# Another written-out order for a fused sliding-window attention and token mixer on one core

## The chip, the core and the metric

The kernel runs on one core of one Trainium2 chip. The metric is the device time of one execution in microseconds (us); a time below is the median of several runs where it says so. The engines are TensorE (PE in the profile, with its weight loads as PEld), VectorE (DVE), ScalarE (ACT), GpSimd (POOL) and SyncE (SP). TensorE's results go to PSUM, which the kernel takes as four pairs of banks, `pair` 0 to 3.

## The reference

Inputs are q, k and v of shape (8 batches, 8 heads, 576 positions, 64), the weights `w_q` and `w_k` (512 x 64) and `w_out` (512 x 512); the output is (8, 576, 512), all in float32. Attention looks back over a window of 128 positions, with a bias that is linear in the distance; a mixer over the positions of each batch follows.

```python
scores = scale * np.matmul(q, k.transpose(0, 1, 3, 2))      # scale = 1/8
bias = slopes[:, None, None] * (-np.abs(rel))[None]         # slopes 2**-(h+1)
mask = (rel >= 0) & (rel < 128)
scores = np.where(mask, scores + bias[None], -1000000000.0)
attn = exp(scores - max) / sum
x = (attn @ v), heads side by side                          # (8, 576, 512)
wq, wk = x @ w_q, x @ w_k                                   # (8, 576, 64)
W_tok = scale * np.einsum('bsd,btd->bst', wq, wk)
mixed = np.einsum('bst,btd->bsd', W_tok, x)
out = np.maximum(mixed, 0.0) @ w_out
```

## The kernel before

**The work of one batch.** The loads bring q, k and v into SBUF as fp16 (the DMA converts). TensorE transposes q (TQ), k (TK) and the last 64 rows of both (TT, for two batches at once); copies bring the transposed blocks from PSUM to the tile `qkT` (ETQ, ETK, ETT). Batch 0 has forms of its own for its first blocks: float32 loads by the queues of ACT and SP (LF), transposes TF and TJ, copies EF and EJ. For each of four groups of 128 keys, g, and each half of the heads, u, QKb.g.u makes the scores in a pair of banks, and EXPb.g.u on ACT writes their exponential to a tile `pt`; MULb.g on DVE multiplies both halves by the exponential of bias and mask, made once at the start. PVb.t multiplies by v, with a column of ones that gives the sums; RC takes their reciprocal and X the product, both on DVE. So one batch is eight QK, eight EXP, four MUL, and five each of PV, RC and X.

**The mixer of two batches.** It works on the pairs of batches (0, 1), (2, 3), (4, 5) and (6, 7), and an operation is named after the first of the two. XT and XTT transpose x, EXT and EXTT copy it out; WQ, WK and WT project it, with copies EWQ, EWK and EWT; G multiplies wk by x (copy EG), MX that by wq, so that the matrix of 576 x 576 is never made. RM and RMT are the relu. OUTb.t multiplies by `w_out` (five for a batch, the last, OUTb.4, for both batches of the pair), EO copies the result to an SBUF tile `osb`, and DO stores it. The very last output, OUT7.3, is made in two halves, a and b.

**What sets the order.** The program keeps no schedule of its own: a function declares each operation with what it depends on, and `ORDER`, one long text, lists all of them in the order of issue. A word such as `ETQ5:D` names the operation and the engine; `TQ5:P3` puts a product on TensorE into the pair 3, and `OUT7.4:P11` into the second bank of pair 1. `Order.follow` reads the text, and each engine has its operations in that order; between engines the semaphores follow from the data and the banks. An engine therefore waits at an operation whose data isn't there, with everything behind it. Copies that may run on ACT or DVE get their engine from the text, and `cp` writes them (L245 for ACT, L247 for DVE; where both sides are fp16, ACT is given pairs of values as float32). EXP, MUL, RC and X always have the same engine, and so the loads L378 to L404, which POOL issues one after the other to one DMA queue.

**Tiles.** There are three sets of buffers for k, two for q, four for v, six `pt`, two `qkT`, 20 `osb`. A load into a buffer waits for the last user of what it held. The stores of the first two pairs of batches all go through SP, and in both orders they stand behind DO3.0, one of the last of them: they are held until then.

**Zero products.** `WARM` gives the sizes of groups of products of a zero tile (WM.0 and on) whose results nobody reads; the order puts them where it likes on TensorE.

Of the kernel before, what the change touches and what calls it, by code (L numbers as in the profile page):

```python
# [15 lines left out]
S = 576  # L16
D = 64
# [46 lines left out]
QK2.1.0:P2 ETT2:D Lv2.1:G EXP2.1.1:A ETT3:D WK0:P10 MUL2.0:D Lv2.2:G EXP2.1.0:A XTT0:P0 QK2.3.0:P3
EXTT0:D WQ0:P11 Lv2.3:G EWK0:A MUL2.1:D EXP2.3.0:A QK2.3.1:P0 TQ3:P2 Lq4.0:G MUL2.2:D EXP2.3.1:A
Lwo0:G WT0:P10 ETQ3:D PV2.0:P0 EWT0:A Lwo1:G TK3.0:P3 ETK3.0:A G0:P10 RC2.0:D Lk4.1:G X2.0:D
MUL2.3:D EWQ0:A Lk4.0:G TK3.1:P3 EG0:A QK3.0.0:P0 EXP3.0.0:A Lv3.0:G ETK3.1:D MX0.0:P1 QK3.0.1:P2
RM0.0:D MX0.1:P3 EXP3.0.1:A Lv3.1:G MX0.3:P0 Lq5.01:G RM0.3:D RM0.1:A PV2.1:P1 QK3.1.0:P2 RC2.1:D
PV2.2:P3 EXP3.1.0:A X2.1:D MX0.2:P0 RC2.2:D QK3.3.1:P1 RM0.2:A X2.2:D PV2.3:P2 Lq5.02:G MUL3.0:D
QK3.1.1:P3 EXP3.3.1:A XT2.0:P00 PV2.4:P01 RC2.3:D EXP3.1.1:A Lq5.03:G X2.3:D TQ4:P1 RC2.4:D EXT2.0:A  # L70
X2.4:D QK3.2.1:P3 ETQ4:D OUT0.2:P20 Lq5.00:G EXP3.2.1:A XT2.1:P21 Lv3.2:G MUL3.1:D EO0.2:A
QK3.2.0:P1 TK4.0:P3 Lv3.3:G EXP3.2.0:A QK3.3.0:P0 ETK4.0:D OUT0.1:P20 Lk5.0:G EXT2.1:D EXP3.3.0:A
QK4.0.1:P1 MUL3.2:D QK4.1.1:P3 Lk5.1:G OUT1.3:P21 EXP4.1.1:A Lv3.4:G MUL3.3:D PV3.0:P0 EO0.1:A
PV3.1:P3 Lk4.3:G EXP4.0.1:A OUT1.1:P20 RC3.1:D RC3.0:D X3.1:D Lk4.2:G EO1.3:A QK4.1.0:P1 X3.0:D
TQ5:P3 EXP4.1.0:A Lt2:G MX0.4:P0 XT3.0:P21 ETQ5:D RMT0:A PV3.2:P1 EO1.1:A PV3.3:P0 Lv5.0:G RC3.2:D
EXT3.0:A X3.2:D OUT1.2:P20 Lv4.0:G RC3.3:D X3.3:D QK4.0.0:P1 TK5.0:P3 Lv4.1:G EXP4.0.0:A XT3.1:P21
ETK5.0:D PV3.4:P00 Lk5.3:G EO1.2:A QK5.1.0:P3 RC3.4:D QK5.0.1:P1 X3.4:D EXP5.1.0:A OUT0.0:P20
Lv4.2:G EXT3.1:D MUL4.0:D EXP5.0.1:A QK5.0.0:P0 Lk5.2:G TK4.1:P3 OUT0.3:P21 EXP5.0.0:A Lk6.0:G
ETK4.1:D TT4:P1 EO0.0:D EO0.3:A Lq6.02:G XTT2:P3 QK5.1.1:P0 ETT5:D ETT4:A OUT1.0:P20 EXTT2:D Lk6.2:G
EXP5.1.1:A MUL4.1:D PV4.0:P3 Lk6.1:G QK4.2.0:P1 EO1.0:A QK4.2.1:P0 RC4.0:D WK2:P21 EXP4.2.0:A X4.0:D  # L80
Lv5.1:G MUL5.1:D OUT1.4:P20 EXP4.2.1:A Lk6.3:G PV4.1:P1 MUL5.0:D EWK2:A Lq6.01:G EO1.4:A TK5.1:P0
# [6 lines left out]
TK7.0:P1 QK6.1.0:P3 Lv5.4:G ETK7.0:D OUT3.3:P20 EXP6.1.0:A RC4.4:D Lv5.3:G X4.4:D QK6.1.1:P1
MUL5.2:D QK6.2.1:P0 QK6.2.0:P3 Lv7.3:G EXP6.1.1:A OUT2.1:P21 Lk7.2:G EXP6.2.0:A XT5.0:P10 OUT2.3:P11
Lk7.3:G EO2.1:A EXT5.0:D EXP6.2.1:A MUL5.3:D PV5.2:P3 Lv6.2:G OUT2.2:P10 EO3.3:A Lv6.0:G RC5.2:D  # L90
EO2.3:A X5.2:D TT6:P2 EO2.2:A TQ7:P0 Lv6.1:G ETT6:D QK6.0.1:P3 ETT7:D QK6.0.0:P1 ETQ7:D Lv6.3:G
EXP6.0.1:A PV5.4:P20 OUT3.2:P21 Lv6.4:G EXP6.0.0:A RC5.4:D MUL6.1:D QK6.3.0:P0 Lv7.0:G PV5.3:P3
EXP6.3.0:A OUT3.1:P10 X5.4:D Lv7.4:G RC5.3:D EO3.2:A X5.3:D Lv7.2:G QK6.3.1:P0 EO3.1:A QK7.1.0:P2
# [59 lines left out]
def kernel(  # L153
# [915 lines left out]
```

## Time and profile before

| | |
|---|---|
| time, median of 3 runs | 136.86 us (136.12 to 137.25) |
| the profiled execution | 136.26 us, of which the span of the trace 134.2 us |
| granted TensorE clock | 1.00 |
| busy TensorE | 122.3 us |
| busy VectorE | 114.1 us |
| busy ScalarE | 103.2 us |
| busy GpSimd (issuing the loads) | 86.3 us |
| first exponential to last exponential | 10.09 to 104.23 us |
| PV7.0, one of the last products of the attention | 109.91 us |
| last product on TensorE | ends at 130.16 us |

Times within the trace count from the start of the span. A row of a group gives the line, the engine, the operation, the written tile, the read tiles and the number of instructions, then the busy time and the mean in ns of one, then the idle time of the engine just ahead of them and what ended most of it. A row of the timeline gives the start, the length, the engine, the line, and the instruction, with how many follow each other. A row of stretches gives for each engine, in the order PE, PEld, DVE, ACT, POOL, its busy time and its instructions, and then the granted clock, the mean number of busy DMA engines and the GB/s. Lines are those of the kernel before.

### The profile page before, as it was taken

What the parts mean: (1) busy time and instruction counts of PE and PEld (TensorE: products, weight loads), DVE (VectorE), ACT (ScalarE), POOL (GpSimd) and SP (SyncE); (2) the same over time, 40 slices, a digit from 0 to 9 for tenths busy, and PEclk for the clock granted to TensorE, in tenths of its full rate; (3) what the DMA queues carried; (4) which work ended last, traced back from release to release, by engine and by line L of the source; (5) the groups of instructions that cost most, each with busy time, mean ns of one, the idle gap of its engine ahead of it and who ended that gap; (6) DMA issues with size and microseconds to landing.
All of it is one profiled execution on the core that took longest, in us unless ns stands there. A gap on an engine that the chain in (4) does not pass through costs nothing.

```text
span 134.2 us, 5053 instructions
## 1 busy us (share of the span) xinstructions
PE 122.3 (91%) x2176; PEld 77.2 (58%) x2176; DVE 114.1 (85%) x197; ACT 103.2 (77%) x145; POOL 86.3 (64%) x108
## 2 busy tenths in 40 slices
PE   6988767889999799999999999999999999999970
PEld 2545545766676475576576675565685576634440
DVE  5746899999999999998999999699999999557830
ACT  2579898945998898988999999999999931367040
POOL 7997989499999659899999999999000000000000
PEclk9999999999999999999999999999999999999999
DMA  3999999999999999999999999999929895758894
GB/s 90 222 171 171 157 154 178 167 158 153 162 165 159 195 188 155 157 154 157 154 157 155 157 158 152 152 155 153 100 88 358 317 363 215 230 151 323 275 364 150
DMA packets 105414, 24.97 MB, mean 186 GB/s; under 512 B 95536, under 2 KB 100912, under 8 KB 105392
## 3 DMA queue, kind: packets, MB, share of 16 engines
q0 software_dynamic: 96832, 14.42, 151.6%
q1 hardware_dynamic: 6688, 9.44, 20.7%
q10 hardware_dynamic: 1872, 0.79, 2.2%
q8 instruction: 17, 0.28, 0.8%
q14 instruction: 5, 0.04, 0.1%
HBM read 29.62 MB, written 9.44 MB: 291 GB/s over the span
## 4 chain that ended last, share of the span: by engine, by line
PE 59%; DMA 16%; DVE 9%; ACT 6%; POOL 3%; issue 3%; ACTq 0%; POOLq 0%; DVEq 0%
PE pair L231 48%; DMA natq<-in_q_dram 12%; PE pair L234 11%; DMA natk<-in_k_dram 4%; ACT pt L654 4%; DVE pt L666 3%; DVE qkT L247 3%; DVE rm L882 2%; POOL natk L378 1%; DVE x L727 1%; ACT rm L880 1%; POOL vt L404 1%; POOL natq L382 1%; ACT wqT L245 0%; ACT gs L245 0%
## 5 line engine op out<-in xcount | busy, mean ns | idle before, releaser
L654 ACT ACTIVATE pt<-pair 128x1024 f16<-128x1024 f32 x64 | 62.9, 1032 | 8.0 <-PE pair L231 7.6
L666 DVE TENSOR_TENSOR pt<-pt,bias 128x2048 f16<-128x2048 f16 x32 | 38.5, 1217 | 0.4 <-ACT pt L654 0.3
L404 POOL DMA_DIRECT2D vt<-in_v_dram x40 | 35.1, 949 | 2.4 <-DMA vt<-in_v_dram 1.2
L231 PE MATMUL pair<-wout_sb,rm 128*128 128x512 f16 (+1 forms) x132 | 31.7, 373 | 0.0
L378 POOL DMA_DIRECT2D natk<-in_k_dram x31 | 28.5, 943 | 2.3 <-DMA natq<-in_q_dram 1.7
L231 PE MATMUL pair<-vt,pt 128*128 128x65 f16 (+1 forms) x576 | 22.2, 194 | 2.2 <-DVE pt L666 0.6
L231 PEld LDWEIGHTS <-pt 128*128 128x128 f16 (+1 forms) x576 | 19.2, 100 | 8.0 <-issue 3.5
L245 ACT COPY osb<-pair 128x512 f32<-128x512 f32 (+1 forms) x24 | 13.9, 593 | 11.4 <-PE pair L231 5.8
L727 DVE TENSOR_TENSOR x<-pair,inv 128x512 f16<-128x512 f32 x32 | 21.8, 690 | 0.9
L231 PE MATMUL pair<-qkT 64*128 64x256 f16 (+2 forms) x320 | 22.1, 250 | 0.4 <-DVE qkT L247 0.2
L247 DVE COPY qkT<-pair 128x1024 f16<-128x1024 f16 (+2 forms) x27 | 19.4, 736 | 3.6 <-PE pair L234 3.5
L231 PEld LDWEIGHTS <-rm 128*128 128x128 f16 x132 | 11.4, 97 | 12.1 <-issue 2.2
L231 PEld LDWEIGHTS <-qkT 64*128 64x128 f16 x320 | 10.6, 94 | 8.3 <-issue 2.8
L247 DVE COPY osb<-pair 128x512 f32<-128x512 f32 (+1 forms) x13 | 8.7, 668 | 5.1 <-PE pair L231 5.1
L390 POOL DMA_DIRECT2D natq<-in_q_dram x12 | 11.1, 949 | 1.8 <-PE pair L231 1.6
L880 ACT ACTIVATE rm<-pair 128x1024 f16<-128x1024 f32 x11 | 11.1, 1041 | 0.5 <-PE pair L231 0.3
L234 PE MATMUL pair<-identh,x 128*128 128x128 f16 x128 | 9.9, 220 | 0.0
L231 PE MATMUL pair<-warm 128*128 128x512 f16 x24 | 8.0, 450 | 1.6 <-DVE warm L316 1.2
L234 PEld LDWEIGHTS <-x 128*128 128x128 f16 x128 | 7.5, 98 | 2.3 <-issue 1.3
L247 DVE COPY xT<-pair 128x1024 f16<-128x1024 f16 x11 | 7.5, 686 | 1.2 <-PE pair L234 1.1
L234 PE MATMUL pair<-identh,natk 64*128 64x64 f16 x248 | 6.9, 191 | 1.4 <-ACT qkT L245 0.6
L234 PE MATMUL pair<-identh,natq 128*64 128x128 f16 (+2 forms) x256 | 6.9, 206 | 0.9 <-DMA natq<-in_q_dram 0.9
(68 smaller groups left out, 129.3 us busy)
## 6 DMA issues: line engine op xcount, KB each, us to landing
out_dram<-osb SPq DMA_DIRECT2D x30, 256.0 KB, 3.0
vt<-in_v_dram POOLq DMA_DIRECT2D x32, 128.0 KB, 6.2
natk<-in_k_dram POOLq DMA_DIRECT2D x31, 128.0 KB, 5.9
natq<-in_q_dram POOLq DMA_DIRECT2D x4, 512.0 KB, 7.8
natq<-in_q_dram POOLq DMA_DIRECT2D x12, 128.0 KB, 5.7
out_dram<-osb SPq DMA_DIRECT2D x9, 128.0 KB, 2.4
vt<-in_v_dram POOLq DMA_DIRECT2D x8, 64.0 KB, 5.6
natt<-in_q_dram POOLq DMA_DIRECT2D x4, 128.0 KB, 6.0
```

Source lines behind the costliest of these rows:

```text
L231: hold(nc.tensor.matmul(*a, **k))
L234: hold(nc.tensor.transpose(*a))
L245: hold(nc.scalar.copy(out_ap, in_ap))
L247: hold(nc.vector.tensor_copy(out=out_ap, in_=in_ap))
L378: return lambda: nc.gpsimd.dma_start(out=natk(b, n), in_=k[b, :, P * n:P * n + P, :].transpose([1, 0, 2]))
L390: return lambda: nc.gpsimd.dma_start(out=rows_q(b)[:, r], in_=q[b, :, 0:512, :].rearrange("h (p r) d -> r p h d", r=QR)[r])
L404: return lambda: nc.gpsimd.dma_start(out=vtv(b, t)[:n, :, 0:D], in_=v[b, :, P * t:P * t + n, :].transpose([1, 0, 2]))
L654: nc.scalar.activation(out=pt, in_=two(s.bank).rearrange("p e c -> p (e c)"), func=AF.Exp, scale=SCALE)
L666: nc.vector.tensor_tensor(out=pv, in0=pv, in1=bt, op=ALU.mult)
L727: nc.vector.tensor_tensor(out=x_s[b % NX][qt].rearrange("p (g h d) -> p g h d", g=2, h=4), in0=sums(p)[:, :, :, 0:64], in1=box["inv"].unsq ...
L880: hold(nc.scalar.activation(out=out_ap, in_=in_ap, func=AF.Relu, scale=WSCALE))
L882: hold(nc.vector.tensor_scalar(out=out_ap, in0=in_ap, scalar1=0.0, scalar2=WSCALE, op0=ALU.max, op1=ALU.mult))
```

## The change

`ORDER` is another text for the same operations, and `WARM` has three groups of zero products, 15 in all, where there were eight, 24 in all. All line numbers behind `ORDER` grow by one. Nothing else differs.

- **First loads.** LF0.0.0.0 goes from ACT's queue to SP's and LF0.0.1.0 the other way. The other first blocks of batch 0 (TF0.1.0) are transposed first, and the zero products stand behind the first of these transposes: seven, then two and six later, where twelve stood around TF0.0.0 and twelve, singly or in pairs and threes, further on.
- **Copies.** From DVE to ACT go ETQ1, ETQ3, ETQ4 and ETQ5; ETK2.0, 2.1, 5.0, 5.1, 7.0 and 7.1; ETT5 and 6; EXT0.0, 1.1, 4.1, 5.1, 6.0 and 7.0; EXTT2; RM0.0 and 0.3; EWT6 and EWQ6; eight EO. From ACT to DVE go EF0.1.0, ETT0 and ETT4, EXT2.0 and 6.1, EXTT4, RM0.1, 0.2 and 6.0, EWQ0, EWQ2 and EWT2, EG6, and nine EO with both halves of OUT7.3 then on DVE. A fill of a constant tile changes its place too.
- **Loads.** POOL issues the same 96 loads in another order. Lk1.0 is the first, Lv2.4 goes from the first place to the 43rd, and the slices of the queries of batches 5 to 7 (Lq) and the tails (Lt) stand elsewhere among the others.
- **The end.** The MULs of batch 7 come in the order 1, 3, 2, 0 instead of 1, 0, 3, 2, and EXP7.0.0 is the last EXP where EXP7.2.0 was; XTT6 and WT6 come behind PV7.1; the OUTs of the last two batches have another order, and DO7.0 and DO7.1 are issued by ACT's queue and not by SP's, DO7.2 by ACT's as before.

The diff, cut to its core:

```diff
@@ -42,72 +42,73 @@
...
-WARM = (6, 6, 1, 1, 2, 3, 3, 2)
...
-LF0.1.0.1:S Lv2.4:G ones.1:D Lq0.2:G pads:D Lk0.2:G wmc:D WM.0:P31 TF0.0.0:P00 WM.1:P31 Lk0.1:G
...
-PV7.2:P3 EXT6.1:A PV7.3:P2 EWT6:D OUT4.2:P00 RC7.2:D X7.2:D PV7.0:P1 OUT5.3:P01 RC7.3:D RC7.0:D
-X7.3:D PV7.1:P3 X7.0:D XT7.1:P20 RC7.1:D OUT4.3:P10 X7.1:D EO5.3:D XT7.0:P11 EO4.3:A OUT4.1:P21
...
-EO7.0:A OUT7.3b:P10 DO7.0:S EO7.1:A OUT7.3a:P11 EO7.3b:D DO7.1:S DO7.3b:A EO7.3a:A DO7.3a:S
...
+WARM = (7, 2, 6,)
...
+Lk1.0:G LF0.1.0.1:S wmc:D Lk0.2:G Lq0.2:G ones.3:D bias:A TF0.1.0:P00 WM.0:P30 Lk0.1:G EF0.1.0:D
...
+OUT7.3a:P20 DO6.1:S EO7.2:A OUT7.3b:P31 EO7.3a:D DO7.2:A EO7.3b:D DO7.3a:S DO7.3b:A
...
```

What stands where, at three places. First ACT's rows about batch 5's first copies, in the kernel before; `pt` is written by an EXP, `osb` by an EO, `qkT` by a copy of transposed q or k, `xT_123` by EXT3.0.

```order
L654 ACTIVATE pt_100<-pair_139 128x1024
L245 COPY osb<-pair_140 128x512
L654 ACTIVATE pt_99<-pair_141 128x1024
L654 ACTIVATE pt_98<-pair_139 128x1024
L654 ACTIVATE pt_98<-pair_138 128x1024
L245 COPY osb<-pair_140 128x512
L245 COPY qkT_74<-pair_139 128x8x32
L654 ACTIVATE pt_99<-pair_138 128x1024
```

The same place in the kernel after:

```order
L655 ACTIVATE pt_101<-pair_141 128x1024
L246 COPY osb<-pair_139 128x512
L246 COPY qkT_75<-pair_140 128x2x4x128
L246 COPY osb<-pair_139 128x512
L246 COPY qkT_75<-pair_138 128x2x4x2x32
L246 COPY xT_123<-pair_139 128x4x128
L655 ACTIVATE pt_98<-pair_138 128x1024
L655 ACTIVATE pt_98<-pair_140 128x1024
```

ETQ5 (128x2x4x128) and ETK5.0 (128x2x4x2x32) now stand among the EXPs of ACT; before, both stood on DVE.

The second place is POOL's row of loads about the tails of batches 4 and 5, Lt2, which go to `natt_90`. Before:

```order
L378 DMA natk_85<-in_k_dram 128x8x64
L378 DMA natk_84<-in_k_dram 128x8x64
L398 DMA natt_90<-in_q_dram 64x16x64
L398 DMA natt_90<-in_k_dram 64x16x64
L404 DMA vt_93<-in_v_dram 128x8x64
L404 DMA vt_92<-in_v_dram 128x8x64 x2
L378 DMA natk_89<-in_k_dram 128x8x64
```

And after:

```order
L379 DMA natk_85<-in_k_dram 128x8x64
L379 DMA natk_84<-in_k_dram 128x8x64
L405 DMA vt_95<-in_v_dram 64x8x64
L379 DMA natk_89<-in_k_dram 128x8x64
L405 DMA vt_92<-in_v_dram 128x8x64 x2
L399 DMA natt_90<-in_q_dram 64x16x64
L399 DMA natt_90<-in_k_dram 64x16x64
```

The tails stand behind one k and two v loads that followed them before; counted from the first load they have 59 ahead of them where there were 56.

The third place is the end of ACT's row: the last copies, and the stores that ACT's queue issues. Before:

```order
L880 ACTIVATE rm_135<-pair_138 128x8x4x32
L245 COPY osb<-pair_139 128x512
L987 DMA out_dram<-osb 128x512
L245 COPY osb<-pair_139 128x512
L245 COPY osb<-pair_141 128x512
L955 DMA out_dram<-osb 128x256
L245 COPY osb<-pair_139 128x256
```

After:

```order
L246 COPY osb<-pair_141 128x512
L988 DMA out_dram<-osb 128x512
L246 COPY osb<-pair_141 128x512
L246 COPY osb<-pair_140 128x512
L246 COPY osb<-pair_141 128x512
L988 DMA out_dram<-osb 128x512
L246 COPY osb<-pair_140 128x512
L988 DMA out_dram<-osb 128x512
L956 DMA out_dram<-osb 128x256
```

The last copy of a half output (128x256), EO7.3a, is gone from ACT, which ends with the store of a half (DO7.3b); two more stores are issued there.

More of the change, by code (lines that the diff above doesn't have):

```diff
@@ L64 @@
[L64 to L81, printed above, removed]
@@ L88 @@
[L88 to L93, printed above, removed]
@@ new lines @@
+MX4.4:P3 X6.4:D RM4.1:D RMT4:A QK7.0.0:P2 DO2.3:S MX4.3:P1 EXP7.0.0:A DO3.1:S OUT5.4:P30 MUL7.2:D
+RM4.3:A MX4.2:P0 MX4.0:P2 PV7.4:P31 RM4.2:D EO5.4:A PV6.3:P1 RM4.0:A DO5.4:S XT6.0:P30 RC6.3:D
+PV7.2:P0 X6.3:D EXT6.0:A OUT4.3:P20 DO2.2:S MUL7.0:D OUT4.2:P30 RC7.2:D X7.2:D PV7.3:P1 EO4.2:A
+RC7.4:D OUT4.1:P21 EO4.3:A RC7.3:D X7.4:D X7.3:D DO4.3:S PV7.0:P3 EO4.1:A PV7.1:P0 DO2.0:S RC7.0:D
+X7.0:D OUT5.3:P10 DO4.2:S RC7.1:D DO4.1:S X7.1:D XTT6:P3 EO5.3:A XT7.1:P21 XT6.1:P20 DO5.3:S
+EXT7.1:A XT7.0:P10 EXT6.1:D OUT4.0:P11 EXT7.0:A EXTT6:A WK6:P10 EO4.0:A DO4.0:S WT6:P11 EWK6:A
```

93 lines of the change are left out of this document (57 added, 36 removed).

## The prediction

> **What bounds the kernel now.** I read the page first, then the busy time of chosen stretches, then the chain of waits, then single loads and the end in the timeline. The page: the engines' shares, the 40 slices of VectorE and ScalarE, and the queue of the loads.
>
> ```profile
> PE 122.3 (91%) x2176; PEld 77.2 (58%) x2176; DVE 114.1 (85%) x197; ACT 103.2 (77%) x145; POOL 86.3 (64%) x108
> DVE  5746899999999999998999999699999999557830
> ACT  2579898945998898988999999999999931367040
> q0 software_dynamic: 96832, 14.42, 151.6%
> ```
>
> VectorE (DVE) is nearly full from slice 6 to slice 32, ScalarE (ACT) a little less so, and both are partly idle in the last eight slices. All loads go through one queue, q0. Next, the busy time per engine (in the order PE, PEld, DVE, ACT, POOL) from the first to the last exponential (EXP), from the first bias product (MUL) to the last normalisation (X7.1), and from PV7.0 to TensorE's last product:
>
> ```profile
> 10.09:104.18 94.09, 88.03 (x1853) 58.87 (x1851) 89.04 (x142) 85.79 (x116) 76.88 (x91) 1.00 2.13 163
> 12.06:112.87 100.81, 94.78 (x1949) 63.28 (x1944) 96.50 (x158) 88.04 (x120) 74.91 (x89) 1.00 2.03 178
> 109.91:130.16 20.25, 20.25 (x177) 10.51 (x175) 13.78 (x23) 7.34 (x11) 0.00 (x0) 1.00 0.76 264
> ```
>
> DVE idles 100.81 − 96.50 = 4.31 us between its first MUL and X7.1; ACT idles 94.09 − 85.79 = 8.30 us between its first and last EXP. In the last stretch TensorE (PE) is full and the other two wait for it. The chain of waits (start, length, what) has loads at the start and PE at the end:
>
> ```profile
> 5.24 7.63 DMA natq<-in_q_dram
> 18.01 7.94 DMA natq<-in_q_dram
> 94.50 10.41 PE pair L231 x216
> 113.55 16.18 PE pair L231 x124
> ```
>
> Between them the loads still set a pace. POOL's issues from the timeline, the landing times of two groups of loads, and TQ7, the user of the last queries:
>
> ```profile
> 86.05 7.70 POOL L404 DMA_DIRECT2D vt<-in_v_dram  x9
> L378 POOL DMA_DIRECT2D natk<-in_k_dram x12: 878/913/989, 53.4 to 75.1; - x12
> DMA to landing us min/median/max: 5.4/5.8/6.6
> L398 POOL DMA_DIRECT2D natt<-in_k_dram x1: 857/857/857, 58.8 to 58.8; - x1
> DMA to landing us min/median/max: 6.3/6.3/6.4
> 80.17 1.92 POOL L390 DMA_DIRECT2D natq<-in_q_dram  x2
> 87.39 0.63 PE L234 MATMUL pair<-identh,natq 64*128 64x64 f16 x32
> ```
>
> One 128 KB load goes out every 7.70 / 9 = 0.86 us and lands six to seven places later, so a load's landing is set by its place in the queue. The last query slices were issued at about 81.0; with such a load's 5.4 to 6.6 us they landed at 86.4 to 87.6, and TQ7 ran at 87.39. So up to 88 us work is done about when its data come; behind that, DVE and then PE set the end.
>
> **The change, part by part.** *Copies to ACT.* Up to the last EXP, ACT gains four ETQ, six ETK, three EXT and one RMT, and loses four EO, two EWQ and one EWT. Means by form (after the bar: busy us, mean ns), the exponentials, and two of them back to back:
>
> ```profile
> L654 ACT ACTIVATE pt<-pair 128x1024 f16<-128x1024 f32 x64 | 62.9, 1032 | 8.0 <-PE pair L231 7.6
> L245 ACT COPY osb<-pair 128x512 f32<-128x512 f32 x23 | 13.5, 602 | 10.6 <-PE pair L231 5.8 <-DVE osb L247 4.9
> L245 ACT COPY xT<-pair 128x512 f32<-128x512 f32 x5 | 3.0, 602 | 0.0
> L245 ACT CAST wqT<-pair 128x512 f16<-128x512 f32 x3 | 1.8, 603 | 0.0
> L245 ACT CAST wkt<-pair 64x128 f16<-64x128 f32 x6 | 1.6, 260 | 0.0
> L880 ACT ACTIVATE rmt<-pair 128x512 f16<-128x512 f32 x2 | 1.3, 637 | 0.0
> L245 ACT COPY qkT<-pair 128x1024 f32<-128x1024 f32 x1 | 1.0, 1020 | 0.0
> L245 ACT COPY qkT<-pair 128x512 f32<-128x512 f32 x1 | 0.6, 585 | 0.1
> L247 DVE COPY qkT<-pair 128x1024 f16<-128x1024 f16 x14 | 9.5, 687 | 0.9 <-PE pair L234 0.8
> L247 DVE COPY osb<-pair 128x512 f32<-128x512 f32 x12 | 8.3, 688 | 3.6 <-PE pair L231 3.6
> L247 DVE COPY qkT<-pair 128x2048 f16<-128x2048 f16 x6 | 7.3, 1220 | 1.0 <-PE pair L234 1.0
> 100.87 1.96 ACT L654 ACTIVATE pt<-pair 128x1024 f16<-128x1024 f32 x2
> ```
>
> Two EXPs of 1.03 us end to end took 1.96, so each operation in a full queue costs its mean less 0.10. Gained: 4 × 0.92 + 6 × 0.485 + 3 × 0.50 + 0.54 = 8.6 us. Lost: 4 × 0.50 + 2 × 0.50 + 0.63 (EWT's two wkt pieces and a small third) = 3.6. ACT's work from first to last EXP becomes 85.8 + 5.0 = 90.8 us. DVE loses four ETQ, six ETK and, net, four EXT up to X7.1 (4 × 1.14 + 10 × 0.61, the rows less 0.08: 10.6 us) and gains five EO, two EWQ and one fill of a constant (7 × 0.61 + 0.3 = 4.6): 96.5 − 6.0 = 90.5. From 12.06 that ends at 102.6 without waits, ten before the 112.87 of now: DVE stops being the bound, and ACT takes its place.
>
> A rule speaks against this. The Trainium skill, "ScalarE: Activation LUTs", Rules for kernel authors, sends simple elementwise work to VectorE, and the same page's price is 186 ns plus 0.833 ns an element. By it an ETQ of 2048 fp16 values would take ACT 1.89 us and an ETK or EXT 1.04, and ACT would gain some 12 us instead of 5. This trace disagrees: the kernel hands ACT two fp16 values as one 4-byte element, and the copy takes 1.02 against DVE's 1.22.
>
> *Start.* The zero products before the first transposes go; TF0.1.0 is first, and seven follow it.
>
> ```profile
> 1.20 2.74 PE L231 MATMUL pair<-warm 128*128 128x512 f16 x6 [1.20 <-DVE warm L316]
> L234 PE MATMUL pair<-ident,osb 128*128 128x128 f32 x12 | 2.9, 388 | 0.0
> 10.09 3.77 ACT L654 ACTIVATE pt<-pair 128x1024 f16<-128x1024 f32 x4 [0.82 <-PE pair L231]
> ```
>
> The first six took 2.74 us, 0.46 each. If the seven are as slow they take 3.2; with the first load in at about 3.5 (estimate: TF0.0.0 follows this row at 3.94) they fill PE from 4.1 to 7.3; the ten fp32 transposes left, at 2.9 / 12 = 0.24, end at 9.7, and the first QK stands behind them. Bounds 9.0 (products at 0.22, as in the last rows below) and 10.6; I take 10.0, beside the row's 10.09. On why they are slow, the Trainium skill, "TensorE: Matmul & The Clock Gate", Part 1, says that the array runs at half rate until about 3.4 us of activity; by it all seven fall into the slow time, which is the case priced above. The later single zero products filled gaps in PE; nothing waits for their result, and I take their loss as 0 (bounds: a gain of 0.2 us for each that stood ahead of ready work, at most 2; and the last rival's loss).
>
> *Load order.* The same 96 loads, so the last one lands when it does now. What counts is the work behind each. The tails of batches 4 and 5 (Lt2) move from 56 to 59 loads ahead of them: 3 × 0.86 later than 58.8 + 6.4 = 65.2, so 67.8. Behind their user TT4 ACT has, counted from the order, 23 EXP and four RM (0.93 each), six EO (0.50) and fourteen others (0.28 to 0.63, together some 6.7) up to its last EXP's end: 35 us. So the last EXP cannot end before 102.8. That is 2.0 us of waiting in all (10.0 + 90.8 = 100.8). DVE, the full engine of now, waited 4.31. I take 2.8, nearer to the floor, since the waits for loads are within DVE's figure too. Last EXP ends at 103.6; now at 104.2. The one load whose buffer comes free late is Lq5.00, behind TQ3 (both near 43); with six loads in the queue, a wait of POOL of up to 5 us would not empty it, and I price it at 0.
>
> *End.* The last rows of the attention, and the last stores:
>
> ```profile
> 103.15 1.08 ACT L654 ACTIVATE pt<-pair 128x1024 f16<-128x1024 f32 x1
> 109.91 0.42 PE L231 MATMUL pair<-vt,pt 128*128 128x65 f16 x8
> 111.03 0.65 PE L231 MATMUL pair<-vt,pt 128*128 128x65 f16 x16
> 112.94 0.61 PE L234 MATMUL pair<-identh,x 128*128 128x128 f16 x8
> 123.08 7.08 PE L231 MATMUL pair<-wout_sb,rm 128*128 128x512 f16 x36
> 130.22 0.36 ACTq L955 DMA_DIRECT2D out_dram<-osb  x1
> 130.68 0.37 ACT L245 COPY osb<-pair 128x256 f32<-128x256 f32 x1 [0.77 <-DVE osb L247]
> ```
>
> Eight OUTs' worth of products take 7.08, 0.88 each. After the last EXP, MX4.0 may use its bank; then PV7.4, PV6.3, XT6.0, PV7.2, OUT4.3, OUT4.2, PV7.3, OUT4.1 stand before PV7.0: 3 × 0.88 + three PV at 0.5 + 0.3 + 0.47 + 0.2 = 5.1, and PV6.3 waits 0.5 for RM4.3, which ACT does behind that EXP: 5.6 (now 109.91 − 104.23 = 5.7). From PV7.0 to the end it is 134.2 − 109.91 = 24.3 now. Two OUTs fewer stand there (−1.76); one XT (+0.47), XTT6 and WT6 (+0.6) are new; RM6.0 moves behind RM6.1 on DVE and holds the first of the last OUTs by about 0.25; and the last copy, which now stands on ACT behind the store issue of 130.22, goes to DVE with nothing but a copy ahead (130.22 − 130.68 = −0.46). That is 23.4.
>
> Sum: 103.6 + 5.6 + 23.4 = 132.6 us of span against 134.2, −1.6. The profiled execution took 136.26, 0.60 under the median of 136.86, so the time is 136.86 − 1.6, about 135.2.
>
> **Rivals.** *ACT becomes worse than DVE was* (slower). All its new copies wait for PE, as the EXPs do (7.6 of its 8.0 us). If it idles 8.3 us as now, the last EXP ends at 109.0 and the span is 138.0: 140.6. Above 5.8 us of idling it is slower by 1%. For it: DVE was nearly as full and could be kept at 4.3. Against: much of the 8.3 was slack that nothing needed. *Nothing moves* (the loads set the pace): no time is gained up to PV7.0, and the end gains its 0.9 or loses as much as 0.5: 136.0 to 137.4. For it: TQ7's row; against: DVE was full behind 88 us too. *Better*: with both engines below DVE's old load, and the tails landing 2 us ahead of my 67.8, ACT would wait 1 us at most: 130.8, so 133.4. *The clock drops*: without products in PE's gaps from 15 to 33 us the pace could fall to the start's 0.46 us again; if 1.5 to 3 us of work then take twice as long, 136.7 to 138.2. Against it: PE was busy for 88 of the 94 us from the first EXP on.
>
> **How the numbers follow.** Less than 1% (135.5 to 138.2) can't be told from no change here. The forecast case has 0.58: waits from 2.0 to 4.3 and 0.6 either way at the end give 133.8 to 137.2, 0.36 of it faster by over 1%, 0.22 within. ACT's idling 0.14, slower; nothing moves 0.12, within; better 0.11, faster; the clock 0.05, 0.03 of it slower. Faster 0.47, within 0.36, slower 0.17. The range from 132.6 to 138.0 leaves out most of the slower case and a little below.
>
> **What would show it.** Right: ACT busy for 90 to 91 us from its first EXP to its last and idle for about 2.8; the last EXP ends near 103.6, PV7.0 follows 5.6 us later, and no copy stands behind the last store's issue. Wrong: a first EXP after 10.6, ACT idle for over 5 us, the tails landing after 69, or PE waiting after PV7.0 for over 1.5 us.

## The result and the profile after

The changed kernel takes 138.01 us (median of 8 executions, 137.56 to 139.18) against 136.92 us for the kernel before (8, 136.12 to 137.25): a ratio of 1.0101, with a 95% interval from 1.0063 to 1.0140. It is slower by 1%, where 135.2 us was forecast. A median takes in every execution; a ratio leaves out those that were over 1.5% above the fastest of their kernel. The profiled execution took 137.83 us, of which 136.1 us are the span.

First the page of the kernel after: the engines' shares and the 40 slices.

```profile
PE 121.0 (89%) x2167; PEld 79.2 (58%) x2167; DVE 108.1 (79%) x188; ACT 109.6 (81%) x154; POOL 86.2 (63%) x108
PE   0999765989998899999999999999998999999960
DVE  6637688888879979999999988899999997078350
ACT  2938997599899999989899989999999945834410
PEclk9999998699999999999999999999999999999999
```

Its groups of instructions by form have the zero products:

```profile
L232 PE MATMUL pair<-warm 128*128 128x512 f16 x15 | 5.2, 498 | 0.0
```

The zero products take 5.2 us where those of before took 8.0; DVE is emptier and ACT fuller. New is the row PEclk: in slices 7 and 8 of 40, from 20 to 27 us, it is below full speed, where it was full throughout before. The busy times by stretch (PE, PEld, DVE, ACT, POOL, then the clock) from the first to the last exponential and from PV7.0 to the last product of the kernel after:

```profile
9.82:106.36 96.54, 89.64 (x1846) 61.27 (x1840) 86.21 (x142) 90.76 (x121) 77.14 (x92) 0.98 2.13 176
111.85:131.41 19.56, 19.56 (x209) 10.69 (x207) 10.94 (x17) 9.72 (x18) 0.00 (x0) 1.00 0.54 198
```

ACT works for 90.76 us, 90.8 were forecast, but idles for 5.78 and not 2.8. Stretches from the start to the last product, first of before, then of after:

```profile
0.00:30.00 30.00, 23.99 (x411) 15.64 (x413) 23.45 (x49) 22.50 (x31) 26.10 (x38) 1.00 1.89 163
30.00:60.00 30.00, 28.38 (x605) 19.14 (x605) 29.16 (x48) 26.86 (x36) 26.42 (x32) 1.00 2.13 165
60.00:88.00 28.00, 27.78 (x567) 17.77 (x565) 26.08 (x44) 26.18 (x36) 27.99 (x34) 1.00 2.42 155
88.00:130.16 42.16, 42.16 (x602) 24.68 (x596) 35.38 (x60) 27.24 (x42) 5.75 (x8) 1.00 1.06 238
```

```profile
0.00:30.00 30.00, 21.65 (x372) 15.48 (x373) 21.19 (x45) 22.73 (x30) 25.96 (x38) 0.94 1.90 163
30.00:60.00 30.00, 28.48 (x570) 19.55 (x568) 26.85 (x43) 29.02 (x40) 26.02 (x31) 1.00 2.12 165
60.00:88.00 28.00, 27.93 (x589) 18.56 (x586) 25.80 (x47) 26.34 (x35) 28.00 (x34) 1.00 2.39 153
88.00:131.41 43.41, 42.89 (x647) 25.58 (x644) 33.86 (x55) 31.55 (x51) 6.27 (x8) 1.00 1.06 229
```

This is the reading that was missed. From 30 us to its last product PE stands idle for 1.62 + 0.22 + 0 = 1.84 us in the kernel before, and for 1.52 + 0.07 + 0.52 = 2.11 in the kernel after. No relief of DVE or ACT can gain more than these 2 us there. Up to 30 us PE idles for 6.01 us before and 8.35 after. Most of that difference costs nothing: ahead of the first exponential PE idles for 1.80 us before and 3.55 after, since the first zero products are gone, and yet the first exponential comes no later (10.09 and 9.82 us). From there to 30 us it is 4.21 and 4.80, and part of PE's work after runs at half the clock. And behind the last product come 134.2 − 130.16 = 4.04 us before and 136.1 − 131.41 = 4.69 after. The slow clock and the longer end are the losses of the change. The fall of the clock in single microseconds of the kernel after:

```profile
22.00:23.00 1.00, 0.41 (x16) 0.29 (x15) 1.00 (x2) 0.77 (x3) 1.00 (x3) 0.90 1.93 194
23.00:24.00 1.00, 0.71 (x14) 0.71 (x14) 0.93 (x3) 1.00 (x2) 1.00 (x2) 0.50 1.48 183
24.00:25.00 1.00, 1.00 (x21) 0.90 (x20) 0.50 (x3) 0.21 (x1) 1.00 (x2) 0.50 1.57 190
25.00:26.00 1.00, 1.00 (x22) 0.80 (x19) 0.96 (x4) 0.62 (x1) 1.00 (x2) 0.50 2.12 166
26.00:27.00 1.00, 1.00 (x30) 0.84 (x27) 0.96 (x3) 0.70 (x2) 0.29 (x1) 0.89 2.35 156
```

The clock is at 0.50 from 22.8 to 26.2 us. The mean clock of the 8 executions is 0.954 to 0.987, none at 1.00; the 137 executions of the kernel before that ran beside the experiments have a mean of 0.995.

### The profile page after: what moved, and what is told of

It reads as the page before. It is cut to its first block, busy times and chain, and to the rows that moved or that the text cites. A ratio compares the mean times of both kernels' runs of the same rounds, so it can differ in the third digit from the quotient of the medians.

```text
span 136.1 us, 5028 instructions
## 1 busy us (share of the span) xinstructions
PE 121.0 (89%) x2167; PEld 79.2 (58%) x2167; DVE 108.1 (79%) x188; ACT 109.6 (81%) x154; POOL 86.2 (63%) x108
## 4 chain that ended last, share of the span: by engine, by line
PE 71%; ACT 16%; DMA 4%; DVE 3%; issue 2%; SPq 0%; ACTq 0%; DVEq 0%
PE pair L232 56%; PE pair L235 14%; ACT pt L655 11%; DMA osb<-in_q_dram 2%; DMA out_dram<-osb 2%; ACT rm L881 1%; ACT qkT L246 1%; ACT wk L246 1%; DVE osb L248 1%; DVE pt L667 1%; DVE qkT L248 1%; DVE x L728 1%; ACT osb L246 0%; ACT xT L246 0%; ACT rmt L881 0%
## 5 line engine op out<-in xcount | busy, mean ns | idle before, releaser
L232 PE MATMUL pair<-wout_sb,rm 128*128 128x512 f16 (+1 forms) x132 | 31.2, 373 | 0.0
L379 POOL DMA_DIRECT2D natk<-in_k_dram x31 | 29.7, 989 | 1.0 <-DMA natk<-in_k_dram 0.5
L232 PE MATMUL pair<-vt,pt 128*128 128x65 f16 (+1 forms) x576 | 22.9, 198 | 1.3 <-ACT qkT L246 0.9
L246 ACT COPY osb<-pair 128x512 f32<-128x512 f32 x23 | 13.4, 595 | 7.8 <-PE pair L232 7.8
L248 DVE COPY qkT<-pair 128x1024 f16<-128x1024 f16 (+2 forms) x17 | 10.8, 640 | 2.8 <-PE pair L235 2.5
L881 ACT ACTIVATE rm<-pair 128x1024 f16<-128x1024 f32 x10 | 10.1, 1041 | 2.7 <-PE pair L232 2.6
L246 ACT COPY qkT<-pair 128x512 f32<-128x512 f32 (+2 forms) x16 | 10.6, 683 | 0.7 <-PE pair L235 0.5
L235 PE MATMUL pair<-identh,x 128*128 128x128 f16 x128 | 9.0, 219 | 0.0
L718 DVE RECIPROCAL inv<-pair 128x8 f32<-128x8 f32 x32 | 6.4, 202 | 2.4 <-PE pair L232 1.9
L235 PEld LDWEIGHTS <-natq 128*64 128x64 f16 (+2 forms) x256 | 6.4, 104 | 2.6 <-issue 1.9
```

The costliest lines, as they stand in the source:

```text
L232: hold(nc.tensor.matmul(*a, **k))
L235: hold(nc.tensor.transpose(*a))
L246: hold(nc.scalar.copy(out_ap, in_ap))
L248: hold(nc.vector.tensor_copy(out=out_ap, in_=in_ap))
L379: return lambda: nc.gpsimd.dma_start(out=natk(b, n), in_=k[b, :, P * n:P * n + P, :].transpose([1, 0, 2]))
L718: nc.vector.reciprocal(out=box["inv"], in_=sums(p)[:, :, :, 64])
```

## The experiments

Ratios are to the kernel before on the same chip; its medians there lie between 136.41 and 136.92 us, so runs are compared by their ratios. The diffs show only the words of a line that change; `...` stands for what is left out. In the kernels with further products, copies or multiplications, their results are read by nothing.

### The clock

Nine zero products are put into PE's waits of the kernel after, behind TK1.0 and around QK1.2.1. No free bank was there for the second place as the order stood, so QK1.2.0 goes behind QK1.2.1.

```diff
-WARM = (7, 2, 6,)
+WARM = (7, 2, 6, 4, 1, 4)
...
-TK1.0:P3
+TK1.0:P3 WM.3:P10
...
-QK1.2.0:P1 Lv0.3:G RC0.1:D MUL1.1:D QK1.2.1:P0
+WM.4:P11 Lv0.3:G RC0.1:D MUL1.1:D QK1.2.1:P0 WM.5:P10 QK1.2.0:P1
```

> The kernel after with nine more zero products: four behind TK1.0 (at 15.7 us in its trace, where TensorE waits 0.96 us), one in the place of QK1.2.0 and four between QK1.2.1 and QK1.2.0, which now come in this order (at 21.3, where TensorE waits 1.17). Theory 1, the granted clock: the trace of after shows the clock at 0.50 from 22.8 to 26.2 us, behind a stretch with TensorE busy about half the time; with the products there it stays at 1.00, the stretch from 22.8 to 26.2 loses about 1.7 us, and the time falls from 138.0 to 136.3 (135.8 to 136.8). Rival, ScalarE has become the bound whatever the clock does: the clock may be 1.00, but the time stays within 0.5 us of 138.0, since ScalarE waits as long elsewhere.

Measured: 137.13 us, 1.0030 (1.0006 to 1.0054), the clocks 0.991 to 1.000. The same stretch of this kernel:

```profile
22.00:23.00 1.00, 0.92 (x22) 0.49 (x20) 1.00 (x2) 0.77 (x3) 1.00 (x2) 1.00 1.96 172
23.00:24.00 1.00, 0.65 (x21) 0.66 (x22) 0.93 (x3) 1.00 (x2) 1.00 (x2) 1.00 1.50 200
24.00:25.00 1.00, 0.95 (x29) 0.81 (x26) 0.96 (x4) 0.51 (x2) 1.00 (x3) 1.00 1.48 191
```

The clock holds, and 0.71% of the 1.01% go, about 1.0 us; 1.7 were expected. To tell the clock from the other order of two products, the order alone:

```diff
-QK1.2.0:P1 Lv0.3:G RC0.1:D MUL1.1:D QK1.2.1:P0
+Lv0.3:G RC0.1:D MUL1.1:D QK1.2.1:P0 QK1.2.0:P1
```

> The kernel after with QK1.2.1 ahead of QK1.2.0, as in the first experiment, but without its nine zero products. Theory 1 (the granted clock, held up by the products): the clock falls below 1.00 in each execution as it does in the kernel after (0.954 to 0.987), and the time stays at 138.0, within 0.4 us. Rival, the other order of these two products is what gained 0.9 us in the first experiment: the time is 137.1 to 137.4.

Measured: 138.45 us, 1.0159 (1.0120 to 1.0198), the clocks 0.954 to 0.975. The order of the two gains nothing; the products and the clock do. In the profile of this run the clock is at half from 20.6 to 27.4 us, twice as long as in the kernel after. Beside this kernel, which has the same order, the nine products are worth 1.0159 − 1.0030 = 1.29%, or 1.8 us, about what was expected of them. The other way round, the kernel before loses its twelve late products:

```diff
-WARM = (6, 6, 1, 1, 2, 3, 3, 2)
+WARM = (6, 6)
```

> The kernel before without its twelve late zero products (WM.2 to WM.7); the order is the same otherwise. Theory 1: the granted clock falls below 1.00 (0.97 to 0.99), behind the stretch from 13 to 20 us, and the time rises by 0.8 to 2 us, to 137.7 to 138.9. Rival: these products only filled time that nobody needed, and the clock is held up by the other work; the clock is 1.00 and the time within 0.4 us of 136.9.

Measured: 137.30 us, 1.0029 (0.9997 to 1.0061), the clocks 0.963 to 0.987. The row PEclk of its page:

```profile
PEclk9996899689999999999999999999999999999997
```

And two of its stretches:

```profile
13.00:16.00 3.00, 2.48 (x52) 2.17 (x52) 1.29 (x2) 1.73 (x3) 2.70 (x4) 0.70 2.41 158
24.00:28.00 4.00, 3.26 (x56) 2.69 (x58) 3.42 (x6) 2.76 (x3) 2.34 (x5) 0.63 2.33 159
```

The clock falls twice in this execution, and no execution has a mean above 0.987. The time rises by about 0.4 to 0.6 us, less than expected, and the interval just takes in no change. So that the clock falls without these products is shown; what the fall costs in this order isn't, nor why it costs so little.

### Which engine sets the pace

One engine at a time gets more work between 55 and 85 us. Eight zero products for PE, in the kernel before and in the kernel after with the nine products of above; the first of the eight in the kernel before:

```diff
-OUT1.1:P20
+WM.8:P20 OUT1.1:P20
```

> The kernel before with eight more zero products on TensorE, one ahead of each of eight OUTs between 56 and 84 us (OUT1.1, 1.2, 0.0, 0.3, 1.0, 1.4, 3.3, 2.1), in the OUT's own bank: 8 x 0.22 = 1.75 us more work for TensorE and none for the others. Theory 4, TensorE is the bound from 30 us on (in the trace of before its waits from 30 us to its last product are 1.6 us in all, and an OUT, a PV or a QK takes the same time in each stretch): the time rises by 1.5 to 1.9 us, to 138.2 to 138.7. Rival, the prediction's reading that VectorE and the loads bound that stretch: TensorE has room, and the time rises by less than 0.6.

> The kernel after with the nine more zero products of the first experiment (137.1 us) and eight further ones, each ahead of one of eight OUTs between 55 and 82 us: 1.75 us of work for TensorE alone. Theory 4 holds for the kernel after too: the time rises by 1.0 to 1.8 us over 137.1, as the kernel before rose by 1.1 with such products. Rival, in the kernel after ScalarE is the bound of that stretch: less than 0.5.

Six multiplications for DVE in the kernel before (0.35 us each, 2.1 in all, in the profile), and six copies for ACT in the kernel after (0.42 each, 2.5 in all). The lines that declare them (in `ORDER` each stands behind an X or an EO):

```diff
+        add("XD", "", i, 0.0, DVE(0.3), [mkb], lambda o: nc.vector.tensor_tensor(out=scr[:, 0:384], in0=bias[:, 0, 0, 0, :], in1=bias[:, 0, 0, 1, :], op=ALU.mult))
...
+        add("XA", "", i, 0.0, ACT(0.37), [wmz], lambda o: nc.scalar.copy(scr[:, 0:512].bitcast(FP32), warm.bitcast(FP32)))
```

> The kernel before with six more products on VectorE, each of 384 fp16 values of a constant (some 0.29 us by MUL's 1.22 for 2048), behind X3.0, X3.3, X4.0, X4.1, X5.0 and X4.2, between 57 and 76 us: some 1.7 us more work for VectorE alone. The prediction's reading, VectorE is the bound: the time rises by 1.4 to 1.8 us. Theory 4, TensorE is the bound and VectorE has 3 us of idle time there: the time rises by less than 0.7.

> The kernel after with six more copies on ScalarE, each of 256 float32 values of a constant (0.28 to 0.37 us), behind EO1.2, EO0.1, EO1.0, EO1.4, EO3.3 and EO3.2, between 59 and 84 us: some 2 us more work for ScalarE alone. The prediction's reading, ScalarE is the bound of the kernel after: the time rises by 1.6 to 2.1 us, from 138.0 to about 139.8. Theory 4, TensorE is the bound: the rise is below 0.8, and what there is comes from TensorE waiting longer in that stretch than the 1.6 us of now.

| kernel | added work | time | ratio | rise |
|---|---|---|---|---|
| before, PE | 1.75 us | 137.98 | 1.0091 (1.0061 to 1.0122) | 1.1 us |
| after with nine products, PE | 1.75 us | 138.73 | 1.0160 (1.0129 to 1.0192) | 1.8 us over 1.0030 |
| before, DVE | 2.1 us | 137.46 | 1.0041 (1.0014 to 1.0067) | 0.6 us |
| after, ACT | 2.5 us | 138.51 | 1.0108 (1.0064 to 1.0153) | 0.1 us over 1.0101 by the ratios, 0.5 by the medians; 1.1 us over 1.0030 |

The last row can't be read against the kernel after alone, since the clock differs. Its means are 0.981 to 0.994 here, where they were 0.954 to 0.987, and the profile shows no fall before the last product:

```profile
PEclk9999999999999999999999999999999999999995
```

Why it held here isn't known, but the time that this saves hides part of what ACT's work cost. Against the kernel with the nine products, whose clock holds too, the rise is 1.1 us. So in the kernel after PE's work comes through whole and of ACT's under half; in the kernel before it is two thirds of PE's and under a third of DVE's. PE sets the pace in both, but not alone.

### The copies by themselves

Ten copies of q and k go to ACT in the order of the kernel before (ETQ1, 3, 4 and 5; ETK2.0, 2.1, 5.0, 5.1, 7.0 and 7.1, each like the two shown):

```diff
-ETQ1:D
+ETQ1:A
...
-ETK2.0:D
+ETK2.0:A
```

> The kernel before with ten copies of transposed q and k on ScalarE instead of VectorE, as the change has them (ETQ1, 3, 4, 5; ETK2.0, 2.1, 5.0, 5.1, 7.0, 7.1), all else in its place: the change's relief of VectorE by itself. By the prediction's sum the time falls by 0.5 to 1.6 us, since VectorE loses 10.6 us of work and ScalarE gains 6.6. Theory 4: TensorE has hardly a wait to lose behind 30 us, so the time falls by no more than 0.3, or rises by up to 1.5 where TensorE now waits for a copy that stands behind exponentials on ScalarE.

And the six ETK go back to DVE in the order of the kernel after:

```diff
-ETK2.0:A
+ETK2.0:D
```

> The kernel after with six copies of k (ETK2.0, 2.1, 5.0, 5.1, 7.0, 7.1) back on VectorE, everything else in its place. Theory 2, ScalarE has taken VectorE's place as the bound (busy 90.8 of the 96.5 us from its first to its last exponential): it loses 6 x 0.49 = 2.9 us of work there, VectorE gains 6 x 0.61 = 3.7 with about 10 us to spare, and the time falls by 1 to 2.5 us, to 135.5 to 137.0. Theory 1 alone (the clock): these copies do not touch the stretch before 23 us, the clock stays at 0.98, and the time stays within 0.5 us of 138.0.

Measured: 139.68 us for the first, 1.0196 (1.0167 to 1.0226), and 140.45 for the second, 1.0248 (1.0201 to 1.0295). The first is 2.7 us slower than the kernel before, more than any of the expectations allowed, the second 2.0 slower than the kernel after, where a gain was expected: either way an engine is relieved, and it costs. PE's waits between 30 and 88 us (what for; us in all, times, the longest), the longest three of the kernel before and four of the kernel with the ten copies on ACT:

```profile
PE pair L231 <- DVE rm L882: 0.5, 1, 0.5
PE pair L231 <- DVE qkT L247: 0.4, 1, 0.4
PE pair L231 <- ACT pt L654: 0.2, 1, 0.2
```

```profile
PE pair L231 <- ACT wkt L245: 0.9, 2, 0.6
PE pair L231 <- ACT rmt L880: 0.7, 1, 0.7
PE pair L231 <- ACT qkT L245: 0.4, 1, 0.4
PE pair L231 <- DVE rm L882: 0.4, 1, 0.4
```

PE's waits there come to 3.3 us in all, where they were 1.1. PE now waits for results of ACT that come later: EWT's pieces (`wkt`), a relu, the copies themselves. In the other kernel PE's longest wait between 30 and 106 us is for the copies now on DVE, 1.1 us. An order fits its own choice of engines: a copy that comes later than PE needs it is lost time, however idle its engine is on the whole.

### The last stores

In the kernel after eleven stores are issued behind 124 us. EO5.2 and DO5.2 go straight behind EO5.1 and DO5.1, first in the kernel after as it is, then with the nine products, and with those and one edit more (ETQ1, below).

```diff
-EO5.1:A DO5.1:S OUT7.0:P31
+EO5.1:A DO5.1:S EO5.2:A DO5.2:S OUT7.0:P31
...
-EO6.2:D EO5.2:A OUT6.3:P31
+EO6.2:D OUT6.3:P31
...
-EO6.0:A DO5.2:S OUT7.1:P30
+EO6.0:A OUT7.1:P30
```

> The kernel after with EO5.2 straight behind EO5.1 on ScalarE and DO5.2 straight behind DO5.1 on SyncE, which in the trace of after were issued at 127.6 and 124.2 us; the eleven stores behind 124 us end 3.7 us after the last product, against 3.1 for ten in the kernel before. Theory 3, the last stores queue up on the DMA engines: one store of 0.65 us moves ahead into a time when they are half idle, and the time falls by 0.3 to 0.7 us. Rival, the end is the last product plus the fixed time of one store: no change, within 0.2 us.

> The kernel after with the nine more zero products of the first experiment (1.003 of the kernel before) and DO5.2 straight behind DO5.1; ETQ1 stays on ScalarE. If the earlier store is worth what the two runs before it showed (1.0029 to 0.9962, 0.9 us), and ETQ1's engine nothing, the time is 0.994 to 0.999 of the kernel before. If the gain came with ETQ1's place or by the chip, it stays at 1.002 to 1.005.

> The kernel of the run before (the kernel after with nine more zero products and ETQ1 on VectorE, 137.0 us) with EO5.2 and DO5.2 straight behind EO5.1 and DO5.1, as in the run with the stores, now with the clock near 1.00. Theory 3, one store too many stands in the last 7.5 us, in which the DMA engines are full at 0.65 us a store (in the seven executions profiled with the order of before the span ends 4.0 to 4.6 us after the last product, in nine with that of after 4.6 to 4.9): the time falls by 0.3 to 0.6 us, to 136.4 to 136.7. Rival: the stores before these are as late and nothing is gained, within 0.2 us of 137.0.

Measured: alone 138.65 us, 1.0084 (1.0046 to 1.0122), which its clocks of 0.953 to 0.997 blur; with the nine products 136.63, 1.0004 (0.9972 to 1.0036), against 1.0030 without the edit; with ETQ1 too 136.25, 0.9962 (0.9936 to 0.9988), against 1.0029. So the edit is worth 0.35 us in one pair, where the two intervals overlap, and 0.9 in the other, where they don't. Behind the last product the profiles show 0.4 in both: 4.63 and 4.60 us without it, 4.22 and 4.21 with it. In the profile of the edit alone, with the clock at half from 19.1 to 29.3 us, that end is 4.8 us and no shorter than in the kernel after: the gain is shown with the nine products only. The stores of the last microseconds, KB each and the median from issue to landing, of before, of after, and of the kernel with all three edits:

```profile
out_dram<-osb SPq DMA_DIRECT2D x8, 256.0 KB, 2.7
```

```profile
out_dram<-osb SPq DMA_DIRECT2D x6, 256.0 KB, 3.3
out_dram<-osb ACTq DMA_DIRECT2D x3, 256.0 KB, 3.5
```

```profile
out_dram<-osb SPq DMA_DIRECT2D x6, 256.0 KB, 2.7
out_dram<-osb ACTq DMA_DIRECT2D x3, 256.0 KB, 2.8
```

And the last stretches of the kernel after, with the mean number of busy DMA engines as a share of 16 and the GB/s at the end of each row:

```profile
127.50:129.00 1.50, 1.50 (x9) 0.69 (x7) 0.16 (x1) 0.79 (x2) 0.00 (x0) 1.00 0.97 318
129.00:130.50 1.50, 1.50 (x10) 0.70 (x8) 1.23 (x2) 0.00 (x0) 0.00 (x0) 1.00 0.99 382
130.50:132.00 1.50, 0.91 (x9) 0.57 (x6) 0.85 (x2) 0.58 (x1) 0.00 (x0) 1.00 1.07 410
132.00:133.50 1.50, 0.00 (x0) 0.00 (x0) 0.00 (x0) 0.00 (x0) 0.00 (x0) 1.00 1.06 358
```

The stores move 320 to 410 GB/s until 2 us after the last product; at 400 GB/s a store of 256 KB takes 0.65 us, and one that is issued late holds up those behind it. What the other 0.5 us of the pair with ETQ1 are wasn't settled. The last edit of the change, taken alone into the kernel before:

```diff
-EO7.3a:A
+EO7.3a:D
```

> The kernel before with one edit, that of the change at its very end: the last copy, EO7.3a, on VectorE and not on ScalarE, where it stood behind the issue of DO7.3b. By the prediction's sum the copy is 0.46 us earlier, and so is the last store: 0.3 to 0.5 us faster than before. Rival, the store waits in its queue for the stores ahead: no change, within 0.15 us.

Measured: 136.75 us, 0.9989 (0.9958 to 1.0019): no change that can be told. In its profile the last store is issued 0.54 us after the last product, where it was 0.91 in the kernel before, but takes 2.6 us to land instead of 2.2.

### The start

Four runs ask what the first 30 us wait for. ETQ1 goes back to DVE, ahead of MUL0.2, and three zero products ahead of TQ1 go, in the kernel with the nine products:

```diff
-EXP0.1.1:A MUL0.2:D QK0.1.0:P2 ETQ1:A TK1.0:P3 WM.3:P10 Lt0:G ETK1.0:D
+EXP0.1.1:A QK0.1.0:P2 ETQ1:D TK1.0:P3 WM.3:P10 Lt0:G ETK1.0:D MUL0.2:D
```

> The kernel after with the nine zero products of the first experiment, with ETQ1 back on VectorE, ahead of MUL0.2 (which moves behind ETK1.0), and with three instead of six zero products ahead of TQ1, so that TQ1 starts as its load lands (13.0 to 13.3 us instead of 14.0). Theory 6, ScalarE bounds the first 30 us of the kernel after (busy 100% from 12 to 20 us; TensorE waits 3.5 us of its 5 there for ScalarE): ScalarE loses 1.0 us there, and the time falls from 137.1 by 0.3 to 1.0 us, to that of the kernel before or below. Rival, the loads bound it: the time stays within 0.3 us of 137.1.

Measured: 137.02 us, 1.0029 (1.0009 to 1.0050), beside 1.0030: ACT's new copy and the three products together cost nothing that can be seen. Next, the kernel with the nine products, ETQ1 on ACT and six zero products ahead of TQ1, has two instead of seven behind TF0.1.0:

```diff
-WARM = (7, 2, 6, 4, 1, 4)
+WARM = (2, 2, 6, 4, 1, 4)
```

> The kernel after with the nine more zero products of the first experiment, and with two instead of seven zero products between TF0.1.0 and TF0.0.0, which start at 3.55 and 7.01 us while the loads of TF0.0.0 have landed at 4.4. If the first products are what holds the start up, the first exponential moves from 9.9 to 8.2 to 9.0 us, and the time falls from 137.1 by as much as the loads behind allow, 0.3 to 1.0. Rival, the loads set the start (TQ1's lands at 13.3, TQ1 starts at 14.0): the first exponential is earlier, and the time stays within 0.3 us of 137.1; or the granted clock falls, since the seven products are gone, and the time rises by 0.5 to 1.5.

Measured: 137.71 us, 1.0069 (1.0035 to 1.0104). The first exponential starts at 9.00 us, 0.9 earlier, but the six products ahead of TQ1 in its timeline show what takes that back:

```profile
13.26 2.70 PE L232 MATMUL pair<-warm 128*128 128x512 f16 x6
```

The same six in the kernel after:

```profile
12.64 1.47 PE L232 MATMUL pair<-warm 128*128 128x512 f16 x6
```

In the first of these rows a product takes 0.45 us, in the second 0.25: without the seven, PE is still at half its speed at 16 us. (The column of the clock reads 1.00 there: it doesn't show the slow start.) The profiled execution took 139.01 us; the twelve lie between 136.69 and 139.05, and how many of them start so slowly isn't known. Then the kernel before with its first load, Lv2.4, issued behind Lv2.3:

```diff
-LF0.1.0.1:S Lv2.4:G ones.1:D
+LF0.1.0.1:S ones.1:D
...
-WQ0:P11 Lv2.3:G
+WQ0:P11 Lv2.3:G Lv2.4:G
```

> The kernel before with its first load, Lv2.4 (64 rows of v that are used some 40 us later), issued behind Lv2.3 instead, as the kernel after has it: every load from Lq0.2 on goes out 0.8 us earlier up to that place, and nothing else moves. Theory 5, the first 30 us are set by the loads (TQ1 starts at 12.91 in the trace of before, its load lands at 12.87; Lk1.1 lands at 14.55, and TK1.0, which needs it, ends at 14.89): TensorE gets to its dense stretch 0.4 to 0.8 us earlier, and the time falls by as much, to 136.0 to 136.5. Rival: the start is set by the first transposes and the exponentials, and the time stays within 0.2 us of 136.8.

Measured: 136.96 us, 1.0033 (1.0010 to 1.0055), slower, where a gain was expected. PE's row for the second half of the first transposes there, with the wait ahead of it:

```profile
8.02 1.79 PE L234 MATMUL pair<-ident,osb 128*128 128x128 f32 x8 [0.98 <-DMA osb<-in_q_dram]
```

LF0.0.0.1 lands at 7.97 us, and in the kernel before at 6.16: the 512 KB of Lq0.2, now first, go out 0.8 us earlier, and most likely share the DMA engines with the first blocks, from which the early load of a tile that nobody needs yet had kept them apart. Last, the kernel before without the five products at 27.0 and 30.2 us:

```diff
-WARM = (6, 6, 1, 1, 2, 3, 3, 2)
+WARM = (6, 6, 1, 1, 3, 2)
```

> The kernel before without the five zero products of WM.4 and WM.5, which stand at 27.0 and 30.2 us, where TensorE is nearly full. Theory 4 (TensorE is the bound from about 27 us on): the time falls by 0.3 to 1.0 us if the clock stays at 1.00, since 5 x 0.22 = 1.1 us of TensorE's work go, part of them in time in which PV1.3 would wait for its bias product. Theory 1 alone: the clock falls as it did without all twelve, and the time rises by 0.3 or more.

Measured: 136.93 us, 1.0030 (1.0002 to 1.0059), the clocks mostly 0.991 and above. Neither theory foresaw it: no gain, and no fall of the clock as without all twelve. PE waits in their place, and in the profiled execution the queries of batch 1 landed 0.3 us later; the rest is open.

## Why the prediction was wrong

**The bound.** The first step failed: "DVE stops being the bound, and ACT takes its place". The sum was then made along ACT's row. The row for the stretch between the first and the last exponential stood in the prediction, with PE busy for 88.03 of 94.09 us; what wasn't asked is where its 6.06 idle microseconds lie. 4.2 of them lie before 30 us, and behind that PE is as full as DVE. Added work says the same: 1.75 us for PE cost 1.1 and 1.8 us, 2.1 for DVE 0.6. ACT's 2.5 us in the kernel after cost between 0.1 and 1.1. So the work taken off DVE, 6.0 us net by the prediction, had no path to the end.

**The sum's terms.** The first exponential (10.0 forecast, 9.82 in the profile), ACT's work (90.8, 90.76), the step from the last exponential to PV7.0 (5.6, 5.49) and the landing of Lt2 (67.8, 67.47) were right. Two were not. ACT's waits are 5.78 us and not 2.8, over the 5 that the prediction named as a sign of being wrong; the rival "ACT becomes worse than DVE was" put the limit at 5.8. That rival foresaw that ACT would wait for PE, but with ACT as the bound; by the runs above it waits since PE sets the pace, and 2.73 of the 5.78 lie between the first exponential and 30 us, about the fall of the clock. And from PV7.0 to the end it is 24.25 us and not 23.4: the products take 19.56, 19.81 by the prediction's terms, but behind the last of them 4.69 and not 4.04 − 0.46 = 3.58. The last store is indeed issued only 0.49 us after the last product, where it was 0.91; it lands 3.19 us later, where it was 2.19, since stores of the kernel's last 7 us stand ahead of it. The profiles vary here: what comes behind the last product is 4.0 to 4.7 us in eight of them with the order of before, and 4.6 to 4.9 in eight with that of after and its stores. The terms −0.18 − 0.04 + 2.98 − 0.11 + 0.85 give the 3.5 us between 132.6 and 136.1.

**The zero products.** "[N]othing waits for their result, and I take their loss as 0" is the second step that failed. The rival of the clock named what happened, and it had a chance of 0.05. That its range, 136.7 to 138.2 us, holds the measured time is in part luck: it adds 1.5 to 3 us to a forecast whose own gain of 1.6 us did not come. Against it stood "PE was busy for 88 of the 94 us", a mean over a stretch, while the clock follows a few microseconds. Where these lie counts too. In the trace of the kernel after the clock's records begin or step at 9.16, 22.81, 26.22 and 135.45 us, whole multiples of 3.41 us apart, and in that of the kernel before at 5.20 and 134.90. On this grid, the last two stretches of the kernel after ahead of the fall:

```profile
15.98:19.40 3.42, 1.93 (x48) 1.52 (x48) 2.55 (x4) 3.42 (x5) 2.53 (x4) 1.00 2.42 152
19.40:22.81 3.41, 1.85 (x53) 1.37 (x45) 2.78 (x4) 2.73 (x4) 3.38 (x6) 1.00 2.31 160
```

And of the kernel before, its emptiest 3.40 us and the two stretches of its grid that share them:

```profile
14.89:18.29 3.40, 1.83 (x34) 1.21 (x34) 3.40 (x5) 3.35 (x5) 2.83 (x4) 1.00 2.42 157
12.02:15.43 3.41, 2.21 (x59) 1.56 (x53) 2.62 (x3) 2.91 (x5) 2.52 (x4) 1.00 2.43 160
15.43:18.85 3.42, 2.20 (x43) 1.54 (x44) 3.30 (x4) 3.37 (x4) 2.85 (x4) 1.00 2.40 152
```

In the kernel after PE is busy for 56% of the first stretch, behind which the clock held, and for 54% of the second, behind which it fell, with no wait over 1.2 us. The kernel before has 3.40 us that are as empty, but they fall across two stretches of 65 and 64%, and there the clock held. The grid lies elsewhere in each profile, which may be why the clocks of one kernel differ. In the profiles of five other runs the clock fell behind stretches of 50 to 59%, and in one of them it held behind one of 50%: the busy share alone gives no limit, and the runs don't settle what else counts. On this the Trainium skill, "TensorE: Matmul & The Clock Gate", Part 1, says that the clock goes by a free-running window of activity of some 3.4 us, and sums up that idle gaps should not exceed such a window. The trace agrees with the length (0.50 for 3.4 us) and the free-running grid, and not with that summary taken alone: many short waits were enough. That page also says that the point varies from run to run; here the clocks of one kernel lie between 0.954 and 0.987.

**The account.** Of the 1.01%, the zero products account for 0.71%, and the place of one store for some 0.26%, which by itself is not clear of noise. With both put right the kernel after is as fast as the kernel before (1.0004), and with ETQ1 on DVE and three zero products fewer it is the fastest here, 0.9962. What the rest of the new order is worth lies then between nothing and 0.4%, at most a third of the forecast.

## What to carry to other kernels

Before costing the relief of a nearly full engine, look at the idle time of all engines by stretch, TensorE's above all; if a second engine is as full there, the relief is worth at most that engine's waits, and a few microseconds of added work for one engine at a time show which it is. Products whose results nobody reads are no free cut where TensorE waits often: check its busy share in stretches of about 3.4 us, wherever these may begin, and not its mean, before they go. An earlier last store gains only if the DMA engines have room then, so count the stores of the last microseconds against the time of one.

## What was not expected of the hardware

The clock fell to half with TensorE busy for a little over half of 3.4 us, and never fully idle for more than 1.2; it changed only at points of a grid of 3.41 us. At the start the profile's clock column reads 1.00 while a product takes 0.45 us instead of 0.25. Six copies moved off a full ScalarE to VectorE with 10 us of idle time cost 2.0 us. A load that is needed 40 us later, issued first, made the kernel faster by 0.3%, most likely as it kept a large load from the first ones.
